# A fused windowed-attention and leaky-ReLU MLP kernel: one set of row sums moved up, unused matmuls taken out, fills moved between engines

## Chip, cores and metric

The kernel runs on one core of a Trainium2 chip. The metric is device time in microseconds of one execution, median of several runs. A core has TensorE (PE; its weight loads are listed as PEld), VectorE (DVE), ScalarE (ACT), GpSimd (POOL) and SyncE (SP), each with its own in-order queue. Transfers are issued from the queues of SyncE and of GpSimd and carried out by 16 transfer engines that all queues share.

## What is computed

Sliding-window attention (each query sees keys within 32 positions on either side), followed by a two-layer MLP without bias. The reference, cut:

```python
batch, n_heads, seq, head_dim = (8, 8, 576, 64)
scores = scale * np.matmul(q, k.transpose(0, 1, 3, 2))
mask = np.abs(pos[:, None] - pos[None, :]) <= window        # window = 32
scores = np.where(mask, scores, -1000000000.0)
attn = softmax(scores)
x = np.matmul(attn, v)          # then transposed to 4608 tokens x 512
h = x @ w_in                    # 512 x 2048
g = np.maximum(0.01 * h, h)
out = (g @ w_out)               # 2048 x 512, float32
```

## The kernel before

Work goes by batch, and within a batch by pairs of heads (four pairs) and halves of the sequence (288 queries). One unit of attention has a number i: for the first two batches, i // 8 is the batch, (i // 4) % 2 the half and i % 4 the pair. The kernel is scheduled by hand: every engine runs its instructions in the order in which the program text issues them, and semaphores are put in by a framework from the tiles that instructions read and write.

The steps of one unit:

- **transposes** (L306 to L340, a generator; each `next` does the queries or the keys of one pair): TensorE transposes the bf16 queries (`qb`) or keys (`kb`) into PSUM (18 small matmuls per tensor at L319 for batch 0, 6 at L323 for batch 1), and ScalarE copies them out (L331).
- **score** (L408): matmuls into the one score tile `ps` (10 at L419 for batch 0, 5 at L426 for batch 1), the exponential on ScalarE into `e` (L431), then a product with the 0/1 mask into `prob` (L433), on GpSimd except for unit 0, which VectorE does.
- **sums** (L465): two matmuls with a block matrix of ones give each query's row sum in `s` (L454), and VectorE takes the reciprocal (L462). `s` has a single buffer, so the next row sums wait for the reciprocal before them.
- **product** (L470): five matmuls with the values (`vbd`) into `x` (L477); **scaled** (L489): VectorE multiplies `x` by the reciprocal into `xT` (L491), the MLP's input. `x` has a single buffer too.

The MLP works on groups of tokens. For group 0 `h_first` (L561) computes the first four chunks of the hidden layer together, one 128-row part of `xT` at a time, as soon as the part of a pair is there; further chunks come from `h_tile` (L525, matmuls at L515, leaky ReLU on ScalarE at L523). `o_pair` (L593) and `o_tile` (L573) are the second layer.

Batch 0 and batch 1 are prepared in different ways. For batch 0 queries and keys are loaded at the start and cast to bf16 on VectorE, with the keys of pair 3 cast on GpSimd and its queries on ScalarE (`cast_qk`, L265). Batch 1's loads are issued by SyncE behind a one-element memset that GpSimd makes (L75, the marker: SyncE's first load waits for it, and so for everything ahead of it in GpSimd's queue). They land in the same buffers, are cast by VectorE (queries) and GpSimd (keys), transposed, and the keys are placed on the diagonal blocks of `kbd[1]` by `place_keys` (L344). `kbd[1]` and `vbd[1]` must hold zeros outside these blocks, so each of their four pair slices, 128 x 1152 bf16, is filled with zeros once. Before, slice 0 of `kbd[1]` is filled on ScalarE at the start (L683), slice 1 on GpSimd at L728, slices 2 and 3 at L783 and L784; of `vbd[1]`, slices 0 and 1 on GpSimd (L768, L782) and slices 2 and 3 on VectorE (L791). Casting transfers of values (`load_cast_v`, L143) and of the weights (`load_w_in`, L673, `load_w_out`, L676) are issued from GpSimd's queue.

Two helpers issue matmuls whose results nobody reads: `warm_up(n)` (L610), n matmuls of 128 x 128, and `keep_busy(t, lo, n)` (L617), n of 128 x 224.

The stage that the change touches is L682 to L785: batch 0's transposes, scores and sums, the first chunks of group 0, then the rest of group 0 with one half unit of attention (`second_half`, L752) after chunks 4, 8, 12 and 15, and the preparation of batch 1 beside group 1. In group 1, `second_pair(0)` (L770) issues batch 1's first transposes after chunk 7, `second_pair(1)` after chunk 11; pairs 2 and 3 follow in the plan's turns 1 and 5 (L854, L865).

Of the kernel before, what the change touches and what calls it, by code (L numbers as in the profile page):

```python
# [16 lines left out]
def kernel(  # L17
# [15 lines left out]
    nc = tc.nc  # L33
# [83 lines left out]
    def clear_vf(p):  # L117
        r = slice(2 * p, 2 * p + 4)
        nc.gpsimd.memset(vtile[0:W, r, 0], 0.0)
        nc.gpsimd.memset(vtile[128 - W:128, r, 4], 0.0)  # L120
# [11 lines left out]
    qT, kbd, vbd, qz, kz, vw, vw_two = [], [], [], [], [], [], []  # L132
# [10 lines left out]
    def load_cast_v(b, p, heads=range(2)):  # L143

        for a in heads:
            r = slice(64 * a, 64 * a + 64)
            nc.gpsimd.dma_start(
                out=vbd[b % 2][r, p, :, r],
                in_=v[b, 2 * p + a].rearrange("(c p) d -> p c d", p=64),
            )  # L150
# [41 lines left out]
    def make_mask(hf):  # L192
        lo = (32, 64)[hf]
        nc.vector.tensor_copy(out=mask[hf][:, 0], in_=win_f[:, lo:lo + HALF])
        lo = (32, 0)[hf]
        nc.vector.tensor_copy(out=mask[hf][:, 1, lo:lo + 256], in_=win_f[:, 0:256])
# [68 lines left out]
    def cast_qk(b, p, q_eng=nc.gpsimd, k_eng=nc.gpsimd):  # L265
        for eng, src, dst in ((q_eng, qf, qb), (k_eng, kf, kb)):
            if eng is None:
                continue
            if b == 0:
                to, tok = dst[:, p, 0:NB * D], src[b, p]  # L270
            else:
                to = dst[0:96, p].rearrange("p (c a d) -> p c a d", a=2, d=D)
                tok = src[b, p].rearrange("p a (c d) -> p c a d", d=D)
            if eng is nc.scalar:
                eng.activation(out=to, in_=tok, func=AF.Copy)
            else:
                eng.tensor_copy(out=to, in_=tok)  # L277
# [77 lines left out]
    def where(i):  # L355
        return i // 8, (i // 4) % 2, i % 4
# [6 lines left out]
    def score_blocks(i):  # L363
        p, bs = i % NPAIR, blocks_of(i)
        n = 2 * 64 * len(bs)
        lo = 512 * (i % 2)
        sc = ps[:, lo:lo + n].rearrange("p (a w c i) -> p a w c i", a=2, c=2, i=32)
        for w, (b, m) in enumerate(bs):
            tok = qz[b % 2][:, p, m // 3].rearrange("p a (c i) -> p a c i", c=2)
            at = 32 * (m % 3)  # L370
            nc.tensor.matmul(  # L371
                sc[:, :, w], kz[b % 2][:, p, 64 * m:64 * m + 128],
                tok[:, :, :, at:at + 32], start=True, stop=True,
            )
        e = attn.tile([128, 2 * HALF], BF16, name="e")
        nc.scalar.activation(out=e[:, 0:n], in_=ps[:, lo:lo + n], func=AF.Exp, scale=scale)  # L376
        pr = prob[:, i % NPROB].rearrange("p n i -> p (n i)")[:, 0:n]
        nc.gpsimd.tensor_mul(pr, e[:, 0:n], band.rearrange("p w c i -> p (w c i)")[:, 0:n])  # L378
        probs[i] = pr.rearrange("p (a w i) -> p a w i", a=2, i=64)
# [28 lines left out]
    def score(i, masked_by=nc.gpsimd):  # L408
        if i >= OLD:
            return score_blocks(i)  # L410
        b, hf, p = where(i)
        tok = qT[b][:, p, hf * HALF:hf * HALF + HALF]
        if b == 0:

            for a, n_, m in ((0, 0, 0), (1, 1, 0), (0, 0, 1), (1, 1, 1), (0, 0, 2),
                             (0, 1, 0), (1, 0, 0), (0, 1, 1), (1, 0, 1), (1, 0, 2)):
                blk, i0, n = WIN[hf][n_][m]
                r = slice(64 * a, 64 * a + 64)
                nc.tensor.matmul(  # L419
                    ps_v[r, n_, i0:i0 + n], first_keys[p][r, 64 * blk:64 * blk + 64],  # L420
                    tok[r, i0:i0 + n], start=True, stop=True,
                )
        else:
            for n_, blocks in enumerate(WIN[hf]):
                for blk, i0, n in blocks:
                    nc.tensor.matmul(  # L426
                        ps_v[:, n_, i0:i0 + n], kbd[b % 2][:, p, blk],
                        tok[:, i0:i0 + n], start=True, stop=True,
                    )
        e = attn.tile([128, 2 * HALF], BF16, name="e")  # L430
        nc.scalar.activation(out=e, in_=ps[:, P0:P0 + 2 * HALF], func=AF.Exp, scale=scale)  # L431
        pr = prob[:, i % NPROB]
        masked_by.tensor_mul(  # L433
            pr.rearrange("p n i -> p (n i)"), e, mask[hf].rearrange("p n i -> p (n i)"),
        )
        probs[i] = [pr, None, None]
# [9 lines left out]
    def row_sums(i):  # L446

        pr, both, _ = probs[i]
        s = xps.tile([128, 512], FP32, name="s")[:, 0:HALF]
        if both is not None:  # L450
            nc.tensor.matmul(s, ones_bd, both, start=True, stop=True)
        else:
            for n in range(2):
                nc.tensor.matmul(  # L454
                    s, ones_bd, pr[:, n],
                    start=(n == 0), stop=(n == 1),
                )
        probs[i][2] = s

    def inverse(i):  # L460
        r = recip.tile([128, HALF], FP32, name="r")
        nc.vector.reciprocal(r, probs[i][2])  # L462
        probs[i][2] = r

    def sums(i):  # L465
        if probs[i][2] is None:
            row_sums(i)
            inverse(i)
# [56 lines left out]
    def h_tile(g, f, n=1):  # L525

        hs = [mmps.tile([128, 512], FP32, name="mm", tag="mm") for _ in range(n)]
        for cs in (range(DMC - 1), (DMC - 1,)) if n > 1 else (range(DMC),):
            for i, h in enumerate(hs):
                h_mms(g, f + i, h, cs)  # L530
        for i, h in enumerate(hs):
            h_out(g, f + i, h)
# [28 lines left out]
    def h_first(g):  # L561

        hs = [mmps.tile([128, 512], FP32, name="mm", tag="mm") for _ in range(4)]
        yield hs[0]
        for c in range(DMC):
            for f in range(4):
                h_mms(g, f, hs[f], (c,))
            if c == DMC - 1:
                for f in range(4):
                    h_out(g, f, hs[f])  # L570
            yield
# [38 lines left out]
    def warm_up(n):  # L610
        t = xps.tile([128, 512], FP32, name="x")
        for _ in range(n):
            nc.tensor.matmul(
                t[:, 0:128], ones_bd, ones_bd, start=True, stop=True, skip_group_check=True,
            )
# [57 lines left out]
    def load_w_in(f0, f1):  # L673
        nc.gpsimd.dma_start(out=w_in_bf[:, :, f0:f1], in_=w_in_r[:, :, f0:f1])

    def load_w_out(i):  # L676
        c = slice(4 * i, 4 * i + 4)
        nc.gpsimd.dma_start(out=w_out_bf[:, c, :], in_=w_out_r[:, c, :])

    first = transposes(0)  # L680

    for t in (vbd[0][:, 3], kbd[1][:, 0]):  # L682
        nc.scalar.activation(  # L683
            out=t.rearrange("p n j -> p (n j)"),
            in_=zero.to_broadcast([128, NB * 128]), func=AF.Copy,
        )
    cast_qk(0, 0, nc.vector, nc.vector)
    make_mask(0)
    load_cast_v(0, 0)
# [13 lines left out]
    sums(0)  # L703
    cast_qk(0, 3, None, nc.gpsimd)
    next(first)
    warm_up(2)
    next(first)
    cast_qk(0, 3, nc.scalar, None)
    warm_up(4)
    load_w_in(512, 1024)  # L710
    score(2)
    load_cast_v(0, 3, (1,))
    load_w_in(1024, 1536)
    sums(1)
    next(first)
    warm_up(3)
    next(first)
    product(0)
    scaled(0)
# [4 lines left out]
    keep_busy(ps, 0, 3)  # L724
    score(4)
    load_w_in(1536, 2048)
    load_w_out(0)
    nc.gpsimd.memset(kbd[1][:, 1], 0.0)  # L728
    h0 = h_first(0)
    h = next(h0)  # L730
    keep_busy(h, HALF, 3)
# [3 lines left out]
    scaled(2)  # L735
    next(h0)
    score(5)
    for p in range(NPAIR):
        load_qk(1, p, nc.gpsimd if p == 0 else None)
    load_w_out(1)  # L740
# [11 lines left out]
    def second_half():  # L752

        i = state["done"]
        weighted(i)
        if i < 7:
            sums(i + 1)
        if i < 5:
            score(i + 3)
        state["done"] += 1  # L760

    for f in range(4, FFC):
        h_tile(0, f)
        if f in (4, 8, 12):
            second_half()
        if f == 4:
            load_w_out(3)
            nc.gpsimd.memset(vbd[1][:, 0], 0.0)  # L768
    second = transposes(1)
    def second_pair(p):  # L770
        next(second)
# [7 lines left out]

    second_half()  # L780
    cast_qk(1, 0, nc.vector)
    nc.gpsimd.memset(vbd[1][:, 1], 0.0)  # L782
    nc.gpsimd.memset(kbd[1][:, 2], 0.0)  # L783
    nc.gpsimd.memset(kbd[1][:, 3], 0.0)  # L784
    clear_vf(2)  # L785
    cast_qk(1, 1, nc.vector)
    load_cast_v(1, 0)
# [32 lines left out]
    at, t = {1: 0.0}, 0.0  # L820
# [10 lines left out]
    t = at[2] - LEAD + 1.8  # L831
    while len(due) + 8 < NC:
# [3 lines left out]
        t = until  # L836
# [77 lines left out]
```

## Time and profile before

| what | value |
|---|---|
| timed runs | 314.58, 313.51, 314.7 us; median 314.58 us |
| the profiled execution, its own time | 312.3 us |
| its span from first to last instruction | 310.6 us |
| TensorE busy in the window 0 to 10 us | 3.67 us |
| 10 to 20 us | 9.39 us |
| 20 to 30 us | 9.00 us |
| 30 to 40 us | 9.09 us |
| 40 to 50 us | 9.95 us |
| 100 to 200 us | 99.43 us |

The profile's page gives busy time by engine, a strip of 40 slices, the chain of work that ended last, and groups of instructions by line. Timelines list instructions of an engine in order: start, length, engine, line, operation, tiles, and in brackets the idle time before and who ended it. Times are microseconds from the start of the span. L numbers are lines of the kernel before.

### The profile page before, as it was taken

The numbers are of one execution on the slowest core, as the hardware profiler recorded it, in microseconds if no ns is written. First come the engines' busy times: TensorE is split into PE (matmuls) and PEld (weight loads), VectorE is DVE, ScalarE is ACT, GpSimd is POOL, SyncE is SP. The second block draws the span as 40 slices with busy tenths as digits, with TensorE's granted clock in tenths as the row PEclk, the third lists the DMA queues.
The fourth block names the chain that finished last, engine by engine and source line by source line (L and its number), as shares of the span: only waits on it lengthen the run. The fifth ranks groups of instructions, "written<-read, shape, count | busy, mean of one in ns | idle before, by whom it ended". The sixth has DMA issues, their size and how long they took to land.

```text
span 310.6 us, 6914 instructions
## 1 busy us (share of the span) xinstructions
PE 297.4 (96%) x2606; PEld 194.2 (63%) x2635; DVE 227.1 (73%) x300; ACT 202.1 (65%) x419; POOL 203.5 (66%) x256
## 2 busy tenths in 40 slices
PE   2889899999999999999999999999999999999996
PEld 2557665585756858585858595959555555544643
DVE  6688979888779897898789777898679866744000
ACT  6637694382965859585849585848589558842731
POOL 8889799968898989588778357578857522110000
PEclk9999999999999999999999999999999999999999
DMA  7999999997999899989999998895970011001002
GB/s 241 202 151 205 268 221 134 205 226 168 191 205 224 139 274 176 203 165 253 192 176 178 249 234 111 188 206 116 198 139 2 36 68 36 0 34 70 34 26 76
DMA packets 121505, 48.29 MB, mean 155 GB/s; under 512 B 96256, under 2 KB 115968, under 8 KB 121472
## 3 DMA queue, kind: packets, MB, share of 16 engines
q1 hardware_dynamic: 107776, 42.48, 68.2%
q0 software_dynamic: 13696, 5.38, 14.6%
q8 instruction: 20, 0.33, 0.5%
q14 instruction: 13, 0.11, 0.1%
HBM read 36.70 MB, written 9.44 MB: 149 GB/s over the span
## 4 chain that ended last, share of the span: by engine, by line
PE 92%; DVE 3%; DMA 1%; ACT 1%; issue 1%; SPq 0%; ACTq 0%; DVEq 0%
PE mm L515 38%; PE mm L585 37%; PE ps L371 4%; PE mm L601 2%; PE s L389 2%; PE x L389 2%; DMA qf<-in_q_dram 1%; DVE qb L277 1%; DVE r L462 1%; PE s L454 1%; PE tp L319 1%; PE x L477 1%; PE ps L419 1%; PE tp L323 1%; PE ps L426 1%
## 5 line engine op out<-in xcount | busy, mean ns | idle before, releaser
L515 PE MATMUL mm<-xT,w_in_bf 128*128 128x256 bf16 (+3 forms) x956 | 133.1, 294 | 0.2
L585 PE MATMUL mm<-w_out_bf,gT 128*128 128x512 bf16 (+2 forms) x537 | 122.5, 373 | 1.2
L398 DVE RECIPROCAL r<-r 128x256 f32<-128x256 f32 (+1 forms) x56 | 95.0, 1696 | 34.3 <-ACT r L397 33.8
L515 PEld LDWEIGHTS <-w_in_bf 128*128 128x128 bf16 x960 | 91.5, 98 | 29.9 <-issue 0.2
L378 POOL TENSOR_TENSOR prob<-e,band 128x512 bf16<-128x512 bf16 (+1 forms) x56 | 62.5, 1117 | 53.7 <-ACT e L376 52.3
L585 PEld LDWEIGHTS <-gT 128*128 128x128 bf16 x560 | 52.1, 98 | 54.1
L523 ACT ACTIVATE gT<-mm 128x288 bf16<-128x288 f32 (+2 forms) x112 | 50.0, 478 | 12.8 <-PE mm L515 9.9
L376 ACT ACTIVATE e<-ps 128x512 bf16<-128x512 f32 (+1 forms) x56 | 32.4, 579 | 27.6 <-PE ps L371 25.6
L590 ACT ACTIVATE o_sb<-mm 128x512 f32<-128x512 f32 (+2 forms) x35 | 20.5, 585 | 39.3 <-PE mm L585 39.1
L546 ACT ACTIVATE gT<-mm 128x512 bf16<-128x512 f32 x64 | 35.7, 596 | 5.3 <-PE mm L515 3.9
L462 DVE RECIPROCAL r<-s 128x288 f32<-128x288 f32 x16 | 31.2, 1952 | 4.6 <-PE s L454 2.9
L402 DVE TENSOR_TENSOR xT<-s,r 64x256 bf16<-64x256 f32 (+1 forms) x56 | 24.3, 435 | 3.7 <-PE ps L371 0.5
L402 DVE TENSOR_TENSOR xT<-x,r 64x256 bf16<-64x256 f32 (+1 forms) x56 | 24.3, 435 | 3.3
L277 POOL CAST kb<-kf 96x768 bf16<-96x768 f32 (+1 forms) x29 | 23.8, 820 | 4.5 <-DMA kf<-in_k_dram 3.8
L303 DVE COPY set<-kT 64x576 bf16<-64x576 bf16 x48 | 21.4, 446 | 1.8 <-DMA kT<-qb 0.9
L371 PEld LDWEIGHTS <-set 128*128 128x128 bf16 x216 | 16.8, 98 | 9.2
L433 POOL TENSOR_TENSOR prob<-e,mask 128x576 bf16<-128x576 bf16 x15 | 19.2, 1279 | 3.2 <-ACT e L431 2.5
L371 PE MATMUL ps<-set 128*128 128x128 bf16 x216 | 21.2, 219 | 0.0
L282 POOL CAST set<-vbuf 128x640 bf16<-128x640 f32 x24 | 17.2, 716 | 5.9 <-DMA vbuf<-in_v_dram 5.9
L277 POOL CAST qb<-qf 96x768 bf16<-96x768 f32 x24 | 19.6, 818 | 1.6 <-DMA qf<-in_q_dram 1.6
L389 PEld LDWEIGHTS <-set 128*128 128x128 bf16 x432 | 18.0, 98 | 0.5
L283 POOL CAST set<-vbuf 64x512 bf16<-64x512 f32 x24 | 14.6, 610 | 1.5
(95 smaller groups left out, 239.6 us busy)
## 6 DMA issues: line engine op xcount, KB each, us to landing
qf<-in_q_dram SPq DMA_DIRECT2D x32, 288.0 KB, 5.5
kf<-in_k_dram SPq DMA_DIRECT2D x32, 288.0 KB, 6.3
out_dram<-o_sb SPq DMA_DIRECT2D x35, 256.0 KB, 2.5
vbuf<-in_v_dram SPq DMA_DIRECT2D x15, 256.0 KB, 4.6
w_in_bf<-in_moe_w_in_dram POOLq DMA_DIRECT2D x4, 512.0 KB, 7.0
w_out_bf<-in_moe_w_out_dram POOLq DMA_DIRECT2D x4, 512.0 KB, 12.1
vbuf<-in_v_dram SPq DMA_DIRECT2D x10, 192.0 KB, 4.5
set<-in_v_dram POOLq DMA_DIRECT2D x16, 72.0 KB, 5.6
```

The costliest lines, as they stand in the source:

```text
L277: eng.tensor_copy(out=to, in_=tok)
L371: nc.tensor.matmul(sc[:, :, w], kz[b % 2][:, p, 64 * m:64 * m + 128], tok[:, :, :, at:at + 32], start=True, stop=True,)
L376: nc.scalar.activation(out=e[:, 0:n], in_=ps[:, lo:lo + n], func=AF.Exp, scale=scale)
L378: nc.gpsimd.tensor_mul(pr, e[:, 0:n], band.rearrange("p w c i -> p (w c i)")[:, 0:n])
L389: nc.tensor.matmul(x[:, a, w], vw[b % 2][:, p, m, a:a + 2].rearrange("p n d -> p (n d)"), pr[:, a, w], start=True, stop=True,)
L398: nc.vector.reciprocal(r[:, 0:n], r[:, 0:n])
L402: nc.vector.tensor_mul(xT[rows, p, t0:t0 + n].rearrange("p (w i c) -> p w c i", i=32, c=2), x[rows, a].rearrange("p (w c i) -> p w c i", c ...
L462: nc.vector.reciprocal(r, probs[i][2])
L515: nc.tensor.matmul(h[:, 0:n], w_in_bf[:, c, ts(f, 128)], xT[:, c, t0:t0 + n], start=(c == 0), stop=(c == DMC - 1),)
L523: nc.scalar.activation(out=to, in_=h, func=AF.Prelu, alpha=0.01)
L546: nc.scalar.activation(out=gT[:, f - 1:f + 1, t0:t0 + 256], in_=hh.rearrange("p (f t) -> p f t", f=2), func=AF.Prelu, alpha=0.01,)
L585: nc.tensor.matmul(o[:, lo:hi], gT[:, f, t0:t0 + 128], w_out_bf[:, f, lo:hi], start=(f == 0), stop=(f == FFC - 1),)
```

## The change

Three edits, all in the stage named above. The sums of unit 1 are issued ahead of the score of unit 2, instead of after it. The `warm_up(2)` between the query and key transposes of pair 2 and the `warm_up(3)` between those of pair 3 are taken out; the `warm_up(4)` stays. The fills of batch 1's tiles are rearranged: slices 1 and 2 of `kbd[1]` go to ScalarE, behind the exponentials of units 4 and 5; slices 0 and 1 of `vbd[1]` and slice 3 of `kbd[1]` stand together on GpSimd behind the last weight transfer, ahead of the first key cast of batch 1. A GpSimd fill stood between the transfers and the marker before (L728); now none does. Three stood behind the first key cast (L782 to L784); now none does.

```diff
+    def clear_on_act(t):
         nc.scalar.activation(
             out=t.rearrange("p n j -> p (n j)"),
             in_=zero.to_broadcast([128, NB * 128]), func=AF.Copy,
         )
+    clear_on_act(vbd[0][:, 3])
+    clear_on_act(kbd[1][:, 0])
...
     next(first)
-    warm_up(2)
     next(first)
     cast_qk(0, 3, nc.scalar, None)
     warm_up(4)
     load_w_in(512, 1024)
+    sums(1)
     score(2)
     load_cast_v(0, 3, (1,))
     load_w_in(1024, 1536)
-    sums(1)
     next(first)
-    warm_up(3)
     next(first)
     product(0)
...
     score(4)
     load_w_in(1536, 2048)
+    clear_on_act(kbd[1][:, 1])
     load_w_out(0)
-    nc.gpsimd.memset(kbd[1][:, 1], 0.0)
...
     score(5)
+    clear_on_act(kbd[1][:, 2])
     for p in range(NPAIR):
         load_qk(1, p, nc.gpsimd if p == 0 else None)
...
         if f == 4:
             load_w_out(3)
-            nc.gpsimd.memset(vbd[1][:, 0], 0.0)
+            for t in (vbd[1][:, 0], vbd[1][:, 1], kbd[1][:, 3]):
+                nc.gpsimd.memset(t, 0.0)
...
     second_half()
     cast_qk(1, 0, nc.vector)
-    nc.gpsimd.memset(vbd[1][:, 1], 0.0)
-    nc.gpsimd.memset(kbd[1][:, 2], 0.0)
-    nc.gpsimd.memset(kbd[1][:, 3], 0.0)
     clear_vf(2)
     cast_qk(1, 1, nc.vector)
```

More of the change, by code (lines that the diff above doesn't have):

```diff
@@ L680 @@
     first = transposes(0)
-    for t in (vbd[0][:, 3], kbd[1][:, 0]):
+    def clear_on_act(t):
         nc.scalar.activation(
```

## The prediction

> **What bounds the kernel now.** I read the page first, then TensorE's waits over the whole run, then the timelines of the first 45 us engine by engine, and last the chain of waits there. The page:
>
> ```profile
> PE 297.4 (96%) x2606; PEld 194.2 (63%) x2635; DVE 227.1 (73%) x300; ACT 202.1 (65%) x419; POOL 203.5 (66%) x256
> PE 92%; DVE 3%; DMA 1%; ACT 1%; issue 1%; SPq 0%; ACTq 0%; DVEq 0%
> L462 DVE RECIPROCAL r<-s 128x288 f32<-128x288 f32 x16 | 31.2, 1952 | 4.6 <-PE s L454 2.9
> ```
>
> TensorE is busy for 297.4 us of 310.6 and is 92% of the chain that ended last. So an edit on another engine is worth only the TensorE wait that it ends. All those waits are these (total, times, longest):
>
> ```profile
> PE tp L319 <- DVE qb L277: 5.3, 2, 4.4
> PE ps L419 <- ACT kT L331: 1.3, 3, 0.9
> PE s L454 <- DVE r L462: 0.9, 1, 0.9
> PE tp L323 <- DVE qb L277: 0.9, 1, 0.9
> PE ps L621 <- ACT e L431: 0.2, 1, 0.2
> ```
>
> The 5.3 and the 0.9 in the second row lie before the change's first line. What is left is about 2.4 us, all before 38 us. From there to the end nothing waits, so a shift won by 38 us is kept only if nothing later becomes late. TensorE's timeline (start, length, then the idle time before and who ended it; merged lengths include the last matmul's drain, so I use start to start):
>
> ```profile
> 11.14 0.40 PE L613 MATMUL x<-ones_bd 128*128 128x128 bf16 x2
> 11.47 0.69 PE L319 MATMUL tp<-ident,kb 64*64 64x64 bf16 x18
> 12.09 0.61 PE L613 MATMUL x<-ones_bd 128*128 128x128 bf16 x4
> 12.90 0.66 PE L419 MATMUL ps<-set,kT 64*64 64x96 bf16 x10 [0.20 <-ACT kT L331]
> 13.49 0.66 PE L454 MATMUL s<-prob,ones_bd 128*128 128x288 bf16 x2
> 14.09 0.69 PE L319 MATMUL tp<-ident,qb 64*64 64x64 bf16 x18
> 14.71 0.50 PE L613 MATMUL x<-ones_bd 128*128 128x128 bf16 x3
> 15.14 0.69 PE L319 MATMUL tp<-ident,kb 64*64 64x64 bf16 x18
> 15.76 0.64 PE L477 MATMUL x<-prob,set 128*128 128x96 bf16 x5
> 16.57 0.43 PE L419 MATMUL ps<-set,kT 64*64 64x96 bf16 x10 [0.18 <-ACT kT L331]
> 16.93 0.42 PE L454 MATMUL s<-prob,ones_bd 128*128 128x288 bf16 x2
> 17.82 0.45 PE L621 MATMUL ps<-mask,ones_bd 128*128 128x224 bf16 x3 [0.22 <-ACT e L431]
> 19.41 0.42 PE L454 MATMUL s<-prob,ones_bd 128*128 128x288 bf16 x2
> 21.88 0.30 PE L454 MATMUL s<-prob,ones_bd 128*128 128x288 bf16 x1 [0.92 <-DVE r L462]
> ```
>
> The same ten score matmuls take 0.59 us to the next group at 12.90 and 0.36 at 16.57: TensorE's clock comes up close to 16.5. VectorE meanwhile works through one reciprocal per pair:
>
> ```profile
> 10.63 1.96 DVE L462 RECIPROCAL r<-s 128x288 f32<-128x288 f32 x1 [0.61 <-PE s L454]
> 14.20 1.96 DVE L462 RECIPROCAL r<-s 128x288 f32<-128x288 f32 x1 [1.61 <-PE s L454]
> 17.39 1.96 DVE L462 RECIPROCAL r<-s 128x288 f32<-128x288 f32 x1 [0.50 <-PE s L454]
> 33.41 4.67 DVE L277 CAST qb<-qf 96x768 bf16<-96x768 f32 x2
> 40.11 0.56 DVE L277 CAST qb<-qf 96x768 bf16<-96x768 f32 x1
> ```
>
> From 17.39 the chain alternates: reciprocal, row sums (they reuse the one `s` buffer, so wait for it), reciprocal, up to the row sums at 21.88. Whatever moves the reciprocal at 17.39 moves all of it.
>
> **Edit 1 and 2: sums and unused matmuls.** Five unused matmuls go: 0.33 us (11.14 to 11.47) and 0.43 us (14.71 to 15.14). The new order step by step. Keys of pair 2 are transposed from 11.14, the four remaining unused matmuls start at 11.76. The sums of pair 1 now come next, but wait for the first reciprocal: 10.63 + 1.96 = 12.59, so 12.63. Behind that wait stands all of TensorE's queue, the score first. Its reciprocal starts 0.71 later, as at 13.49 to 14.20: 13.34 instead of 14.20. Score of pair 2 follows at 12.63 + 0.59 = 13.22, that is 0.32 later than now; query transposes of pair 3 at 13.81, keys at 14.43 (0.62 each, 14.09 to 14.71), product of pair 0 at 15.05 instead of 15.76. Now ScalarE:
>
> ```profile
> 15.87 0.65 ACT L331 ACTIVATE kT<-tp 128x576 bf16<-128x576 bf16 x1 [0.40 <-PE tp L319]
> 21.07 0.65 ACT L431 ACTIVATE e<-ps 128x576 bf16<-128x576 f32 x1 [1.69 <-PE ps L419]
> 23.45 1.32 ACT L523 ACTIVATE gT<-mm 128x288 bf16<-128x288 f32 x4 [1.73 <-PE mm L515]
> 2.46 2.19 ACT L683 ACTIVATE set<-zero 128x1152 bf16<-128x1152 bf16 x2
> ```
>
> Each copy or exponential takes 0.65. The exponential of pair 2, behind its score's 0.66 and a step of 0.05, runs from 13.93 to 14.58, the query copy behind it to 15.24, the key copy to 15.85 (now 16.52), so score 3 starts at 15.89 instead of 16.57: 0.68 earlier. With the clock coming up at 16.5 as now, that score still runs slowly (0.59, not 0.36), its sums start at 16.48 instead of 16.93, and the reciprocal at 16.94 instead of 17.39. That is **0.45 us**; with both kernels at one speed there it is the 0.68.
>
> The new order of waits on TensorE's own semaphore ahead of the pair 3 transposes has no row here. Its bounds are 0 (what it waits for is older) and 0.2 (one matmul's drain, 0.61 less the 0.4 to be issued at 12.09); I take 0, and it lies in the range.
>
> **Edit 3: the fills.** GpSimd's timeline, and the chain of waits at the cast:
>
> ```profile
> 17.85 1.26 POOL L433 TENSOR_TENSOR prob<-e,mask 128x576 bf16<-128x576 bf16 x1 [0.70 <-ACT e L431]
> 22.21 1.08 POOL L728 MEMSET set<- 128x1152 bf16 x1
> 24.45 0.09 POOL L75 MEMSET qf<- 1x1 f32 x1
> 29.48 1.08 POOL L768 MEMSET set<- 128x1152 bf16 x1
> 33.20 0.82 POOL L277 CAST kb<-kf 96x768 bf16<-96x768 f32 x1 [2.64 <-DMA kf<-in_k_dram]
> 35.96 1.05 POOL L784 MEMSET set<- 128x1152 bf16 x1
> 33.41 4.02 DVE qb L277
> ```
>
> The mask product of score 3, at 17.85 behind 0.70 of idle time, can follow its exponential 0.45 earlier; it ends at 18.7, ahead of the sums that need it at 18.96.
>
> VectorE's cast at 33.41 lasts 4.02 us where the same shape takes 0.56 at 40.11, and it ends, at 37.43, 0.4 us after the last of GpSimd's three fills (35.96 + 1.05 = 37.01). TensorE waits 0.91 us for it at 37.48. Two of the five fills go to ScalarE, 1.1 us each by its row at 2.46, into idle times of 1.69 and 1.73 us: free, with 0.6 to spare; past that each 0.1 us would delay the next exponential by as much. Three stand together at 29.48, where GpSimd then waits 2.64 us for a load: the two extra take 2.1 of it. VectorE there does reciprocals, and their mean of 1952 ns on the page, some of them beside GpSimd's fills, tells of no blocking. So the cast is free of the fills and ends about 34, and the **0.91 us** goes. What is late next is GpSimd's own key cast (0.82), which can hold the cast until about 33.5; the transposes come at 36.1.
>
> The Trainium skill, "SBUF — State Buffer", section "Who interferes with whom", says that VectorE's cast and a GpSimd instruction take a shared port pair whole, and that the first to issue blocks the other. By one such turn the cast would lose 1.05 us; the row shows that it lost all three, 3.46 us, and the sum goes by the row.
>
> GpSimd loses the fill at 22.21, so its mask product and the marker at 24.45, behind which SyncE issues all of batch 1's loads, come about 1.45 us earlier (0.45 by the chain, 1.0 by the fill). This matters later:
>
> ```profile
> 42.15 0.84 POOL L277 CAST kb<-kf 96x768 bf16<-96x768 f32 x1
> 42.84 0.64 PE tp L323 x12
> ```
>
> The key cast of pair 2 of batch 1 ends at 42.99 and its transposes, the second half of the twelve matmuls from 42.84, start at 43.1: no slack. With TensorE 1.36 earlier they come at 41.75, and the load behind that cast must have moved as well. It is issued 1.45 earlier, so I count no loss; if the transfer engines deliver it no sooner, TensorE gives back 0.8 there.
>
> **Sum.** 0.45 + 0.91 = 1.36, say 1.4. The profiled execution took 312.3 us (span 310.6) and becomes 310.9. The median of the three timed runs is 314.58, 2.3 above it, and I carry the difference over: **313.2 us**. About 0.5%, 1.6 us, is what a measurement of this kernel can tell from no change.
>
> **Rivals.**
> 1. *Clock up later.* The unused matmuls kept TensorE at work, and the slow stretch ends just behind them. If full speed comes only at about 20, behind the row sums at 19.41, the steps from 17.82 to 19.41 (1.59 us) stretch by 0.59/0.36 = 1.65 to 2.6; the sums at 19.41 then come at 20.0, 0.6 late instead of 0.45 early. Total −0.3: 314.3. For it: only five groups stand between the score at 12.90 and the speed-up. Against it: the gaps left beside it are no longer than now (0.20 and 0.18). The Trainium skill, "TensorE: Matmul & The Clock Gate", sections "Part 1: The HAM clock gate" and "Part 4: PE-mode transpose", speaks for it: the gate opens after a busy window of some 3.4 us, and transposes do not count as busy. By an estimate from that page the next chance after 16.5 is 19.9.
> 2. *Slower: the clock stays low into the dense stage.* If full speed comes only at 25.7, when TensorE's matmuls run without gaps, the loss grows by about 0.6 by 22.4, where reciprocals still hide part of it, and by half of the 3.3 us after: 0.6 + 0.6 + 1.65 − 0.91 = +1.9: 316.5. It turns slower from a full speed later than about 22. For it: the 0.92 idle before 21.88 stays. Against it: two groups of keep-busy matmuls around 18 remain.
> 3. *Loads not sooner.* −1.36 + 0.8: 314.0. For it: these loads share the transfer engines with the second matrix's weights, issued around them. Against it: the issue itself moves.
> 4. *Clock up earlier*, the sums of pair 1 standing against the unused matmuls: if the steps from 13.2 run fast, ScalarE's copies bound, score 3 starts at 15.6 and its reciprocal at 16.4: 0.97 + 0.91, −1.9: 312.7.
>
> **How the numbers follow.** Forecast 0.50 (312.6 to 313.6: 0.68 instead of 0.45, or the 0.2 drain), rival 1 0.17, rival 2 0.11, rival 3 0.10, rival 4 0.12. Faster by over 0.5%: rival 4 and four tenths of the forecast, whose edge lies at 313.0: 0.32. Slower: rival 2, 0.11. Within: 0.57. The range leaves out rival 2 and the best end of rival 4; rivals 1 and 3 lie in it with half a microsecond of the spread of the shown runs (313.51 to 314.7): 312.2 to 315.0.
>
> **What would show it.** Right: the second reciprocal at 13.3, the reciprocals after it 0.4 to 0.7 earlier, batch 1's first query cast under 1.4 us and no wait of TensorE at the first L323, key casts of pair 2 before 41.7. Wrong: 0.6 us score groups beyond 17, a wait at the third L323 group, exponentials behind the new ScalarE fills.

## Result and the profile after

The changed kernel takes 311.4 us (median of 7 runs, 310.46 to 312.97), before 313.88 us (7 runs, 313.13 to 314.7): a ratio of 0.9925 with a 95% interval of 0.99 to 0.9951, or 2.4 us. The forecast was 1.4 us, and 311.4 lies below the stated range. The profiled execution of the changed kernel took 311.33 us with a span of 309.6, the one of before 312.3 with 310.6: between the two profiles there is only 1.0 us.

TensorE's waits over the whole run, after (total, times, longest):

```profile
PE tp L319 <- DVE qb L277: 5.4, 2, 4.4
PE s L454 <- DVE r L462: 1.3, 2, 0.9
PE ps L419 <- ACT kT L331: 1.1, 2, 0.7
PE tp L319 <- DVE kb L277: 0.2, 1, 0.2
```

The wait at L323 is gone. TensorE's timeline after, in the stage of edits 1 and 2:

```profile
11.97 0.61 PE L613 MATMUL x<-ones_bd 128*128 128x128 bf16 x4
13.00 0.66 PE L454 MATMUL s<-prob,ones_bd 128*128 128x288 bf16 x2 [0.41 <-DVE r L462]
13.59 0.66 PE L419 MATMUL ps<-set,kT 64*64 64x96 bf16 x10
14.04 0.69 PE L319 MATMUL tp<-ident,qb 64*64 64x64 bf16 x18
14.54 0.67 PE L319 MATMUL tp<-ident,kb 64*64 64x64 bf16 x18
15.14 0.64 PE L477 MATMUL x<-prob,set 128*128 128x96 bf16 x5
16.09 0.66 PE L419 MATMUL ps<-set,kT 64*64 64x96 bf16 x10 [0.31 <-ACT kT L331]
18.00 0.43 PE L419 MATMUL ps<-set,kT 64*64 64x64 bf16 x10
21.87 0.42 PE L454 MATMUL s<-prob,ones_bd 128*128 128x288 bf16 x2 [0.91 <-DVE r L462]
```

The row sums at 21.87 stand where they stood before (21.88), so in this pair of profiles the early stage shows no gain at all. Two things hide it. The first reciprocal starts 0.35 us later than in the profile of before (10.98 against 10.63), ahead of every instruction that the change moves. And the slow score group at 16.09 shows that the clock came up later: the trace's record of the granted clock starts at 17.64 us, in before's at 16.50. The casts after on VectorE, then the marker, the fills and the key casts on GpSimd:

```profile
33.03 0.46 DVE L491 TENSOR_TENSOR xT<-x,r 128x288 bf16<-128x288 f32 x1
33.40 0.56 DVE L277 CAST qb<-qf 96x768 bf16<-96x768 f32 x1
34.16 0.56 DVE L277 CAST qb<-qf 96x768 bf16<-96x768 f32 x1 [0.19 <-DMA qf<-in_q_dram]
```

```profile
23.27 0.09 POOL L75 MEMSET qf<- 1x1 f32 x1
29.46 3.07 POOL L771 MEMSET set<- 128x1152 bf16 x3
32.47 0.83 POOL L277 CAST kb<-kf 96x768 bf16<-96x768 f32 x1
33.23 0.32 POOL L119 MEMSET vbuf<- 32x256 f32 x1
37.14 0.82 POOL L277 CAST kb<-kf 96x768 bf16<-96x768 f32 x1 [2.93 <-DMA kf<-in_k_dram]
40.64 0.82 POOL L277 CAST kb<-kf 96x768 bf16<-96x768 f32 x1
```

The first query cast takes 0.56 us instead of 4.02, and the key cast of pair 2 has moved from 42.15 to 40.64.

**Stages of every profile.** To tell stages apart I take starts from the timelines: the first reciprocal (A), from it to the fifth (B: the slow clock and edits 1 and 2), from the eighth reciprocal to the first L323 group (C: the wait for the query cast; 5.43 where there is none), from there to the seventh L323 group (D: waits for the later key casts), and from the first L585 matmul to the end (E). What lies between is the same in all: 7.97 to 7.98 us from the fifth to the eighth reciprocal, 5.17 from the seventh L323 group to L585 (5.22 in the kernel with the sums alone). The column "clock" is where the trace's record starts; in four profiles it is empty.

| kernel | clock | A | B | C | D | E | span |
|---|---|---|---|---|---|---|---|
| before, 1st profile | 16.50 | 10.63 | 12.37 | 6.51 | 9.77 | 258.17 | 310.6 |
| before, 2nd | 19.29 | 11.21 | 12.87 | 6.69 | 9.78 | 258.24 | 311.9 |
| before, 3rd | 20.16 | 11.29 | 13.16 | 6.24 | 9.78 | 258.59 | 312.2 |
| before, 4th | 18.71 | 10.83 | 12.84 | 5.79 | 9.77 | 258.19 | 310.6 |
| before, 5th | | 10.82 | 13.47 | 6.24 | 9.77 | 258.20 | 311.7 |
| before, 6th | 21.21 | 10.93 | 13.85 | 5.43 | 9.64 | 258.70 | 311.7 |
| changed, 1st | 17.64 | 10.98 | 12.01 | 5.43 | 9.64 | 258.42 | 309.6 |
| changed, 2nd | 16.56 | 11.13 | 11.79 | 5.43 | 9.64 | 258.57 | 309.7 |
| changed, 3rd | 14.42 | 10.85 | 11.79 | 5.43 | 9.64 | 258.63 | 309.5 |
| changed, 4th | 18.54 | 10.35 | 12.39 | 5.43 | 9.77 | 259.00 | 310.1 |
| fills alone | 19.14 | 10.76 | 12.97 | 5.43 | 10.03 | 259.18 | 311.5 |
| sums alone | 14.40 | 10.74 | 11.80 | 6.33 | 9.78 | 260.65 | 312.5 |
| no unused alone | 16.25 | 10.22 | 11.87 | 6.44 | 9.78 | 258.17 | 309.6 |
| sums, no unused | 16.14 | 10.42 | 11.79 | 5.43 | 11.09 | 259.22 | 311.1 |
| no unused, fills | | 10.93 | 12.11 | 5.43 | 9.64 | 258.57 | 309.8 |
| late loads | 18.39 | 10.55 | 12.27 | 5.43 | 10.02 | 259.14 | 310.6 |
| fills beside | | 10.55 | 12.58 | 5.43 | 9.64 | 258.86 | 310.2 |
| before, early clock | 11.91 | 11.12 | 11.07 | 5.43 | 11.01 | 258.81 | 310.6 |
| changed, early clock | 7.42 | 10.45 | 11.31 | 5.43 | 9.64 | 258.19 | 308.2 |
| no unused, fills, early clock | | 11.30 | 11.07 | 5.43 | 9.64 | 259.34 | 309.9 |

Means of the six profiles of before and the four of the changed kernel: B 13.09 and 12.00, C 6.15 and 5.43, D 9.75 and 9.67, E 258.35 and 258.66, spans 311.4 and 309.7. The gain between these is 1.7 us: 1.1 in B, 0.7 in C, 0.1 in D, less 0.3 in E, the rest in A.

### The profile page after: what moved, and what is told of

It reads as the page before. It is cut to its first block, busy times and chain, and to the rows that moved or that the text cites. A ratio compares the mean times of both kernels' runs of the same rounds, so it can differ in the third digit from the quotient of the medians.

```text
span 309.6 us, 6903 instructions
## 1 busy us (share of the span) xinstructions
PE 296.8 (96%) x2601; PEld 194.2 (63%) x2630; DVE 223.9 (72%) x300; ACT 203.8 (66%) x421; POOL 200.9 (65%) x254
## 4 chain that ended last, share of the span: by engine, by line
PE 83%; DMA 8%; DVE 4%; issue 1%; ACT 1%; POOL 0%; SPq 0%; ACTq 0%; DVEq 0%
PE mm L585 37%; PE mm L515 35%; DMA kf<-in_k_dram 6%; PE ps L371 4%; DVE r L462 3%; DMA set<-in_v_dram 2%; PE s L389 2%; PE x L389 2%; PE s L454 1%; PE ps L419 1%; PE x L477 1%; SPq L81 0%; ACT kT L331 0%; PE ps L426 0%; DVE xT L491 0%
## 5 line engine op out<-in xcount | busy, mean ns | idle before, releaser
L585 PE MATMUL mm<-w_out_bf,gT 128*128 128x512 bf16 (+2 forms) x537 | 122.5, 373 | 1.3
L585 PEld LDWEIGHTS <-gT 128*128 128x128 bf16 x560 | 52.1, 98 | 54.1
```

What stands on the lines that cost most here:

```text
L585: nc.tensor.matmul(o[:, lo:hi], gT[:, f, t0:t0 + 128], w_out_bf[:, f, lo:hi], start=(f == 0), stop=(f == FFC - 1),)
```

## Experiments

Ratios are to before, on the same chip, with 95% intervals; they weigh the runs otherwise than a quotient of the medians does. The theories that the expectations name are told as they come.

**Each edit alone.** Theory A put the missing gain into the fills, theory B into the early stage.

```diff
+    clear_on_act(kbd[1][:, 1])
-    nc.gpsimd.memset(kbd[1][:, 1], 0.0)
+    clear_on_act(kbd[1][:, 2])
-            nc.gpsimd.memset(vbd[1][:, 0], 0.0)
+            for t in (vbd[1][:, 0], vbd[1][:, 1], kbd[1][:, 3]):
+                nc.gpsimd.memset(t, 0.0)
-    nc.gpsimd.memset(vbd[1][:, 1], 0.0)
-    nc.gpsimd.memset(kbd[1][:, 2], 0.0)
-    nc.gpsimd.memset(kbd[1][:, 3], 0.0)
```

> Before with the fills rearranged alone; row sums and unused matmuls stay as they were. Theory A (the fills carry nearly all of the gain, and the cast held up beside them costs more in most executions than the 0.9 us of wait in the one that was profiled): 1.8 to 2.4 us under before, some 311.8. Theory B (the fills give the 0.9 to 1.1 us that the two profiles show between 32 and 37 us, and the earlier row sums the rest): 0.9 to 1.1 us under before, some 312.9. Both: no wait of TensorE at the first L323 group.

312.89 us, ratio 0.9975 (0.9954 to 0.9995): 0.8 us, near theory B's 0.9 to 1.1 and short of theory A's 1.8. In its profile TensorE does not wait at the first L323 group (C 5.43).

```diff
+    sums(1)
     score(2)
...
-    sums(1)
```

> Before with the second row sums ahead of the third score alone; all unused matmuls stay. Theory A: within 0.4 us of before. Theory B: 0.5 to 1.0 us faster. By the working of the prediction: the score is 0.65 us later than in before with the unused matmuls still there, so pair 3's keys are too and nothing is won, 0 to 0.4 slower.

312.41 us median, ratio 0.9974 (0.9947 to 1.0002): inconclusive. The stage B of its profile is 11.80 where before has 12.37 or more, but its clock also came up at 14.40, the earliest of all without added matmuls, so this is not the row sums' work alone. Its runs spread from 311.37 to 315.08, and its profile has waits past 89 us that no profile of before shows at this size (E 260.65).

```diff
-    warm_up(2)
...
-    warm_up(3)
```

> Before without the five unused matmuls alone. Theory A: within 0.4 us of before, the 0.7 us that goes being taken back by a later clock. Theory B: 0.5 to 1.0 us faster. If the unused matmuls kept the clock up: 0.3 or more slower, with score groups of 0.6 us beyond 17 us.

312.09 us, ratio 0.9944 (0.9922 to 0.9966): more than theory B's upper end, and against the notion that the unused matmuls kept the clock up.

```diff
-    warm_up(2)
...
+    sums(1)
     score(2)
...
-    sums(1)
...
-    warm_up(3)
```

> Before with earlier row sums and without the five unused matmuls; the fills stay. Theory A: within 0.4 us of before (the profiled pair stood level at 25 us). Theory B: 1.3 to 1.5 us faster, some 312.5. Both: the cast beside the fills still takes about 4 us and TensorE still waits about 0.9 us at the first L323 group.

312.22 us, ratio 0.9957 (0.9935 to 0.998). The time is near theory B's 312.5, but by luck: it is no faster than without the unused matmuls alone, and the part that both theories shared failed, since the cast was not held up. Its timelines, VectorE, GpSimd, TensorE:

```profile
32.62 0.55 DVE L277 CAST qb<-qf 96x768 bf16<-96x768 f32 x1
35.92 1.34 DVE L277 CAST qb<-qf 96x768 bf16<-96x768 f32 x1 [2.75 <-DMA qf<-in_q_dram]
```

```profile
32.69 1.17 POOL L277 CAST kb<-kf 96x768 bf16<-96x768 f32 x1 [2.92 <-DMA kf<-in_k_dram]
33.80 1.05 POOL L780 MEMSET set<- 128x1152 bf16 x1
37.92 0.82 POOL L277 CAST kb<-kf 96x768 bf16<-96x768 f32 x1
41.62 0.82 POOL L277 CAST kb<-kf 96x768 bf16<-96x768 f32 x1
```

```profile
38.80 0.43 PE L323 MATMUL tp<-ident,kb 96*128 96x96 bf16 x6 [0.29 <-POOL kb L277]
42.50 0.43 PE L323 MATMUL tp<-ident,kb 96*128 96x96 bf16 x6 [0.81 <-POOL kb L277]
```

VectorE arrives at 32.62, 0.07 us ahead of GpSimd's key cast, which waits for its load. Now it is the key cast that is longer (1.17 against 0.82) and the query cast that is short. But the loads are as late as before, the key casts behind them too, and TensorE loses 0.29 + 0.81 us there. This is rival 3 of the prediction at work, at its price of 0.8 for pair 2 and 0.3 more for pair 1.

**The clock.** Theory C said that the clock's rise wanders between executions and was early in the profile of before; theory D that it is the same for all. The early variant adds unused matmuls where TensorE is idle anyway:

```diff
     load_cast_v(0, 1)
+    warm_up(14)
     next(first)
     next(first)
+    warm_up(7)
...
     cast_qk(0, 2, nc.vector, nc.vector)
+    warm_up(7)
     score(1)
```

> Before with 28 further unused matmuls in TensorE's idle times ahead of the first transposes, behind pair 0's, and ahead of the second score, so that its clock comes up early; nothing else is changed. Theory C (the clock's rise falls anywhere between 14 and 20 us from execution to execution, it was early in the profiled execution of before, and a later rise is what the other executions pay): all score groups from 9 us on take under 0.45 us, 1.2 to 2.5 us under before, some 312, and a narrower spread. Theory D (the five unused matmuls simply cost their own time, the clock is the same for all): within 0.5 us of before.

311.72 us, ratio 0.9934 (0.991 to 0.9958), runs from 310.69 to 312.45. In its profile the first score group behind 10 us takes 0.43:

```profile
13.17 0.43 PE L419 MATMUL ps<-set,kT 64*64 64x96 bf16 x10 [0.42 <-ACT kT L331]
13.53 0.42 PE L454 MATMUL s<-prob,ones_bd 128*128 128x288 bf16 x2
```

The expectation had it fast from 9 us on; the group at 9.82 still took 0.66, so the rise came later than meant. Stage B falls to 11.07. And again the query cast got in first and the late loads took back 1.0 us (TensorE's waits at L323 for the key casts):

```profile
PE tp L323 <- POOL kb L277: 1.0, 2, 0.6
```

> The changed kernel with the same 28 unused matmuls in early idle times. Theory C: 0.5 to 1.5 us under the changed kernel, some 310.3, and about 1.2 to 1.6 under the early variant of before, as the fills' 0.9 and a rest of the order stay. Theory D: within 0.5 us of the changed kernel, and 2.4 under the early variant of before.

310.87 us, ratio 0.9921 (0.9893 to 0.995). Less than expected beside the changed kernel's 0.9925, and 0.85 us by the medians under the early variant of before, where theory C had 1.2 to 1.6; neither step is clear of the intervals. Its row sums, moved ahead, wait long once TensorE is fast, and the score stands behind them. The wait is listed under a cast of GpSimd, but the row sums need the first reciprocal, which ends at 10.45 + 1.96 = 12.41:

```profile
12.47 0.42 PE L454 MATMUL s<-prob,ones_bd 128*128 128x288 bf16 x2 [1.19 <-POOL kb L277]
12.81 0.43 PE L419 MATMUL ps<-set,kT 64*64 64x96 bf16 x10
```

With the clock up, stage B takes 11.31 in this order and 11.07 in the old one. That the earlier row sums pay while the clock is low no run shows clearly: with the unused matmuls out alone and the rise at 16.25, B is 11.87; with the row sums moved as well and the rise at 16.14, it is 11.79.

> Before once more, unchanged, for a second profile and the spread. Theory C: the score groups turn from 0.6 to 0.4 us later than the 16.5 us of the first profile, and the span is over 311.3. Theory D: the turn at 16 to 17 us, and what makes the other executions longer stands elsewhere in the timeline.

314.18 us, ratio 1.0005 (0.9982 to 1.0029). Its profile has what theory C asked for: the rise at 19.29 instead of 16.50 and a span of 311.9. Of the 1.3 us more, 0.5 stands in B; 0.6 stands in A, ahead of the first reciprocal. The score and sums that were fast in the first profile are slow in this one:

```profile
17.16 0.66 PE L419 MATMUL ps<-set,kT 64*64 64x96 bf16 x10 [0.18 <-ACT kT L331]
17.75 0.66 PE L454 MATMUL s<-prob,ones_bd 128*128 128x288 bf16 x2
19.35 0.43 PE L419 MATMUL ps<-set,kT 64*64 64x64 bf16 x10
```

**Without the earlier sums:** the edits of the first and third kernel above together.

```diff
-    warm_up(2)
-    warm_up(3)
...
-    nc.gpsimd.memset(kbd[1][:, 2], 0.0)
+    clear_on_act(kbd[1][:, 2])
```

> Before without the five unused matmuls and with the fills rearranged; the second row sums stay behind the third score. If the earlier row sums add nothing beside the others (both theories after the runs so far): as the changed kernel, 311.2 to 311.7. If they carry part of the gain: 0.4 or more over it.

311.43 us, ratio 0.9926 (0.9901 to 0.9951): the changed kernel's figures. The earlier row sums add nothing measurable beside the other two edits: 0.8 us for the fills alone and 1.8 for the unused matmuls alone already make up the 2.3 of this kernel.

**What the fills are worth once TensorE is early.**

```diff
-    clear_on_act(kbd[1][:, 1])
     load_w_out(0)
+    nc.gpsimd.memset(kbd[1][:, 1], 0.0)
```

> The changed kernel with one fill, slice 1 of kbd[1], back on GpSimd ahead of the marker, so that batch 1's loads are issued about 1.1 us later. Theory L (rival 3 of the prediction holds as a mechanism: once TensorE is early, the key casts behind late loads become its wait): waits of 0.3 to 0.8 us at the second and third L323 groups, 0.5 to 1.0 us slower than the changed kernel. Theory M (the loads have slack): no wait there, within 0.3 us of the changed kernel.

311.84 us, ratio 0.9943 (0.992 to 0.9966). The wait is there, but only at the third pair's keys and only 0.2 us; the price by time, 0.4 us beside the changed kernel, is not clear of the intervals. Theory L is right in kind and its size too large.

```profile
PE tp L323 <- POOL kb L277: 0.2, 1, 0.2
```

```diff
-            for t in (vbd[1][:, 0], vbd[1][:, 1], kbd[1][:, 3]):
-                nc.gpsimd.memset(t, 0.0)
+            nc.gpsimd.memset(vbd[1][:, 0], 0.0)
...
     cast_qk(1, 0, nc.vector)
+    nc.gpsimd.memset(vbd[1][:, 1], 0.0)
+    nc.gpsimd.memset(kbd[1][:, 2], 0.0)
+    nc.gpsimd.memset(kbd[1][:, 3], 0.0)
```

> The changed kernel with three fills (slice 1 of vbd[1], slices 2 and 3 of kbd[1]) back behind the first key cast; the loads stay early. Theory L: the key cast and with it the fills come 1.4 us earlier than in before and end near 35.6, so the query cast is held for 2 to 3 us but ends before TensorE asks for it at 36.4; wait 0 to 0.3 us, within 0.4 us of the changed kernel. By the prediction's own step 3: the 0.9 us of wait comes back, 0.9 slower.

311.94 us, ratio 0.9948 (0.9928 to 0.9967). VectorE and GpSimd in its profile:

```profile
33.55 3.50 DVE L277 CAST qb<-qf 96x768 bf16<-96x768 f32 x2
```

```profile
32.16 0.82 POOL L277 CAST kb<-kf 96x768 bf16<-96x768 f32 x1 [1.47 <-DMA kf<-in_k_dram]
32.92 1.05 POOL L783 MEMSET set<- 128x1152 bf16 x1
34.92 1.05 POOL L785 MEMSET set<- 128x1152 bf16 x1
```

The two casts together take 3.50 us: the first is held until the last fill ends (34.92 + 1.05 = 35.97) and ends at 36.4. Yet C is 5.43, no wait: with the loads earlier the cast is over before TensorE asks, at 36.54, though only just. So in these profiles either half of the third edit, loads earlier or fills elsewhere, takes away that wait.

**More profiles of the two kernels, unchanged,** for where the clock rises.

> The changed kernel unchanged, for a second profile. Theory C (the new order lets the clock rise about 2 us earlier on average than the old, at 14 to 18 us against 16 to 20): the rise before 18.0. Theory C' (the rise falls in the same range for both orders): anywhere from 14 to 20. In either, from the first reciprocal's start to the fifth's it takes 11.8 us where the rise is at 16 and 12.1 at 18.

311.42 us; rise at 16.56: theory C. B is 11.79, as expected for a rise at 16.

> Before unchanged, for a third profile. Theory C: the rise after 16.4. Theory C': anywhere from 14 to 20. In either, from the first reciprocal's start to the fifth's it takes 12.4 us where the rise is at 16.5 and 12.9 at 19.

313.89 us; rise at 20.16, B 13.16: theory C.

> Before unchanged, a fourth profile. Theory C (the new order lets the clock rise earlier): the rise after 17. Theory C' (same range for both orders): as likely before 17.5 as after.

312.56 us; rise at 18.71, B 12.84: theory C. Yet the span is that of the first profile, 310.6, since C is 0.7 shorter: a later clock is not paid in full.

> The changed kernel unchanged, a third profile. Theory C: the rise before 18.4. Theory C': as likely after 17.5 as before.

311.32 us; rise at 14.42, B 11.79: theory C.

> The changed kernel unchanged, a fourth profile. Theory C: the rise before 18.4. Theory C': as likely after 17.5 as before.

311.79 us; rise at 18.54, B 12.39: 0.14 us past theory C's bound.

> Before unchanged, a fifth profile. If the longer executions come from the early stages: a time over 313.9 us goes with a fourth-row-sum stretch (first to fifth reciprocal) over 12.9 us or a first reciprocal after 11.2, and the part behind the first second-layer tile stays at 258.2 to 258.6 us. If they come from later waits: that last part is over 259.

313.52 us: B is long (13.47) and E 258.20, but the time is under 313.9, so it tells little of the longer executions.

> Before unchanged, a sixth profile, with the same two outcomes: over 313.9 us with the early stages long and 258.2 to 258.6 us at the end, or with the last part over 259.

313.55 us: the longest B of all (13.85, rise at 21.21), and C 5.43. In the same execution the lateness has eaten the other wait, as TensorE's and VectorE's timelines show:

```profile
38.18 0.42 PE L323 MATMUL tp<-ident,qb 96*128 96x96 bf16 x6
```

```profile
32.75 1.96 DVE L462 RECIPROCAL r<-s 128x288 f32<-128x288 f32 x1
35.19 3.39 DVE L277 CAST qb<-qf 96x768 bf16<-96x768 f32 x2
```

The first of these two casts was over when TensorE came to it at 38.18. Both executions lay close to the median (313.45 for before's other runs on that chip), so what the longest ones of before (up to 316.47) hold isn't seen.

**A version that beats both:** the early matmuls, no unused ones between transposes, the fills rearranged, the row sums in their old place.

```diff
+    warm_up(14)
...
+    warm_up(7)
...
+    warm_up(7)
     score(1)
...
-    warm_up(2)
...
-    warm_up(3)
...
+    clear_on_act(kbd[1][:, 1])
+    clear_on_act(kbd[1][:, 2])
```

> Before without the five unused matmuls, with the fills rearranged and with the 28 early unused matmuls; the second row sums stay behind the third score. If the earlier row sums are worth something only while the clock is low (from the first reciprocal's start to the fifth's, the early variant of before took 11.07 us and that of the changed kernel 11.31): 10.7 to 11.1 us there, and 0.2 to 0.5 us under the early variant of the changed kernel, some 310.4. If they are worth their place at any clock: over 11.3 us, and no faster than it.

310.01 us, ratio 0.988 (0.984 to 0.9919), the lowest of all. B is 11.07 as expected. Its interval still touches the changed kernel's (0.99 to 0.9951), so against before it is sure, against the changed kernel likely.

## Why the prediction was wrong

**What bounds the kernel: right.** TensorE's waits before 38 us, and the matmuls between them, were the place, and nearly all of the gain is there. But "nothing waits" from there to the end did not stay so: in three of the four profiles of the changed kernel the row sums near 52 us wait 0.23 to 0.42 us for a reciprocal, in none of before's. It is most of the 0.3 us that E gives back; the longest, in the fourth profile:

```profile
52.53 0.42 PE L454 MATMUL s<-prob,ones_bd 128*128 128x288 bf16 x2 [0.42 <-DVE r L462]
```

**Edits 1 and 2, the term of 0.45: the chain right, the size not.** Counted from the first reciprocal, the second was to start 2.71 us later and did 2.72 later (13.70 − 10.98); score 3 was to come 5.26 after it and came 5.11; the third reciprocal 6.31 and 6.40. The gain of 0.45 is also what profiles with the clock rising at the same point show: 12.37 against 11.79 in B at 16.5 (0.58), 12.84 against 12.39 at 18.6 (0.45). But the term took the one clock of the one profile for the kernel's. Over all profiles B falls by 1.1, and by time the unused matmuls alone are worth 1.8 us (1.1 to 2.4). Nor does the term say whose gain it is. With the unused matmuls out alone the third reciprocal starts 6.26 us after the first, with the row sums moved as well 6.15 (rises at 16.25 and 16.14), in the first profile of before 6.76. So nearly all of it is edit 2's: the 0.45 us by which edit 1 brings the second reciprocal forward (2.71 instead of 3.16 behind the first) is nearly all lost again while score 3 waits for ScalarE's key copy.

**The other half of it goes with the clock, on the side that I gave 0.12.** With the old early stage the record starts at 16.50, 18.71, 19.14, 19.29, 20.16 and 21.21 us (mean 19.2); with the row sums moved, the unused matmuls out, or both, at 14.40, 14.42, 16.14, 16.25, 16.56, 17.64, 18.39 and 18.54 (mean 16.5). The ranges overlap, so a single pair of profiles can show either sign, as the first pair did, and the difference of the means rests on few profiles. Rivals 1 and 2, a later clock, did not come: taking the unused matmuls out moved the rise forward if anything, and rival 4's direction holds though no step of mine gave its cause. Why these orders bring it sooner isn't settled. The Trainium skill, "TensorE: Matmul & The Clock Gate", section "Part 1: The HAM clock gate", says that the gate watches a free-running window of some 3.4 us, so that the rise varies from run to run and should not be fitted. The variation is here, 4.7 us within one kernel. The estimate of 19.9 for the next chance after 16.5, drawn from that page, took the window of one execution for that of all: rises stand at 18.71 and 19.29 in between.

**The sum: the step that failed, together with the 0.45 in it.** "The median of the three timed runs is 314.58, 2.3 above it, and I carry the difference over." The difference was no constant. The profiled execution of before, 312.3 us, is the bottom of what before does: its later runs reach from 312.26 to 316.47. Its clock rose earlier than in the other four profiles of before that record it, and its first reciprocal was the earliest of the six. The changed kernel's profile stands at its median (311.33 and 311.4). Against the mean of the six it is 0.3 us short in A, 0.7 in B and 0.2 in E, and 0.4 long in C. The 0.7 in B is time that the change takes away, and the sum carried it over. Of the 1.8 us between the forecast and the result, another 0.7 is the baseline: with four more runs the median of before is 313.88, not 314.58. The remaining 1.1 is gain that the sum lacks: in the profiles 0.65 in B and 0.1 in A, less 0.1 in C and D and 0.3 in E, and some 0.7 that no profile shows.

**Edit 3: right, as a bound.** Predicted 0.91; in the profiled pair C falls by 1.08 and on average by 0.7, between 0 and 1.26. It is smaller on average since the wait is not a fixed price: it ends with GpSimd's fills, which follow the load, so a TensorE that is late by the clock waits less, and one that is early gets its cast in ahead of the fills and meets the late key casts instead. That the loads move with GpSimd's queue was right: the marker comes 1.2 us earlier (24.45 to 23.27), not 1.45, since the early stage of that execution had not moved, and pair 2's key cast stands at 40.64, ahead of its transposes at 41.84. The fills on ScalarE took 1.15 us each in its idle times and cost nothing.

The Trainium skill, "SBUF — State Buffer", section "Who interferes with whom", leaves it to the order of issue which of the two engines is blocked. Both outcomes are here: 4.02 us for the query cast behind the key cast, 0.55 ahead of it, when the key cast took 1.17.

**What stays open.** The ten profiles give 1.7 us, the medians 2.4; the interval of the ratio, 1.5 to 3.1 us, holds both. The four profiled executions of the changed kernel average 311.5 us, its median; the six of before average 313.2, 0.6 below theirs. So the rest lies in longer executions of before than those profiled, and what these hold wasn't seen.

## What to carry to other kernels

Set the profiled execution's own time beside the timed median before adding up terms: where it stands at the edge of the runs, some stage in it is not typical, and a difference carried over as a constant can hold time that the change takes away. Three runs are few for a baseline: here four more moved it by half of what was forecast. A clock that rises in a warm-up stage is a variable of each execution; price the stage for an early and a late rise, and test it by filling idle time ahead of it. Time each edit of a group alone: here one of three gave nothing that could be measured. And waits that stand one behind the other on a stream of loads do not add: taking one away shows the next.

## What the runs showed of the hardware

One cast of VectorE was held through the rest of a GpSimd cast and three fills one behind the other, not for one of them: it took 4.02 us and ended 0.4 us behind the last fill. Yet it did not wait for GpSimd's queue to run dry. The next instruction there, a small fill, stood directly behind and was itself longer, 0.71 us where it takes 0.32 in the changed kernel's profile:

```profile
36.96 0.71 POOL L119 MEMSET vbuf<- 32x256 f32 x1
```

In single profiles, the same unused matmuls in idle time brought the clock's rise to 11.91 us in the kernel before and to 7.42 in the changed one, and stage B to 11.07 and 11.31 us, from means of 13.09 and 12.00.
